# Gate and value products of the last two full token chunks as seven 64x64-tile products, sums accumulated on copies in PSUM, issued from a table

## The chip, the cores and the metric

The kernel runs on one core of a Trainium2 chip. The core has a matrix engine (TensorE, **PE** in the profile; PEld is its weight load), a vector engine (**DVE**), an activation engine (**ACT**), a general engine (**POOL**) and a queue that only issues transfers (**SP**). Engines run side by side and wait for one another through semaphores; each executes its own instructions in order. Products land in PSUM, which has eight banks of 128 partitions x 512 fp32; everything else lies in SBUF. The metric is the time of one execution on the device in microseconds.

## The reference, cut to what matters

An attention block with a feature map of 64 products gives `x`; a gated feed-forward block follows. The change touches the feed-forward block alone.

```python
def phi(x):
    a = np.einsum('rd,bhsd->bhsr', S1, x)
    b = np.einsum('rd,bhsd->bhsr', S2, x)
    return np.einsum('bhsi,bhsj->bhsij', a, b).reshape(*x.shape[:-1], r * r)
# batch 4, heads 4, seq 1088, head_dim 32
num = np.einsum('bhsf,bhfd->bhsd', q_p, kv); den = ...
x = (num / den).transpose(0, 2, 1, 3).reshape(4352, 128)

gate = 1.0 / (1.0 + np.exp(-(x @ w_gate)))     # 4352 x 128 by 128 x 1536
val = x @ w_val                                # 4352 x 128 by 128 x 1536
return gate * val @ w_out                      # 4352 x 1536 by 1536 x 128
```

All is fp32.

## The kernel before, in words

**Tiling.** `xT` holds `x` transposed, 128 features on the partitions and 4352 tokens along them. The tokens are cut into nine chunks: 0 to 7 of 512 tokens, 8 of 256. The 1536 hidden units are twelve blocks j of 128. One *wave* (`w1`, L541) is gate and value of one block j for one chunk: on PE four products (L556), each with 128 rows of contraction and 64 output columns, 512 tokens wide. A product with 64 output columns takes half of PE's columns, so two run beside each other. Then one sigmoid on ACT (L564) and one multiplication on DVE (L599), which writes `g`. The wave's PSUM tile has two banks and two buffers (`psm`). Chunk 8 takes two blocks j in a wave, and its multiplication (L592) also reorders its tokens.

**The output product.** For chunks 1 to 7 two waves make a pair i. The product with `w_out` of a pair (two blocks of 128 hidden units, 128 outputs, 512 tokens as two halves) is done in seven products instead of eight: POOL forms four sums of `g` over token halves (`token_sums`, L371, tile `tsum`), sums of the weights are formed once (`ws`), and PE runs seven products of 128 rows x 64 columns x 256 tokens in `w2_a` and `w2_b` (all through `product`, L381), which add up in the banks `acc0` and `acc1`. After the last pair of a chunk ACT and DVE combine the parts (L486 to L529, L496), DVE transposes (L533) and SP stores (L393). For chunk 8 `w2_end` (L451) runs products of 64 columns with 128 outputs along them, into a bank of `acc0` and one of `ps2`, and `store_end` (L403 to L409) copies the two halves, one on ACT and one on DVE, and stores them from ACT's queue and from SP.

**Order.** Nothing is reordered afterwards on PE, DVE, ACT and POOL: they execute as the Python loop emits. A *slot* (L625) emits the multiplication of the previous wave, then what is due of the output products (a pair's `w2_a` three slots after its second wave, `w2_b` four), then the next wave. Attention of batches 1 to 3 is emitted between slots by a plan of wave numbers (L1352 on); wave 72 is the first of chunk 6, wave 84 the first of chunk 7, and attention has ended by then. `slot(None, 10**3)` emits all the rest. The scheduler of the tile layer sets only SP's order.

**Stores.** Every result tile that is stored uses the tag `o_sb` of pool `sbA`, which has two buffers; the two tiles of `store_end` use it too (L405).

Of the kernel before, what the change touches and what calls it, by code (L numbers as in the profile page):

```python
# [14 lines left out]
MUL = ALU.mult  # L15

P = 128


@with_exitstack  # L20
def kernel(
# [20 lines left out]
    assert DM == H * D == P and D == 32 and R == 8 and S % 32 == 0 and NTOK % 512 == 256  # L42

    T = S // 32

    NJK = 9
    KBASE = [0, 9, 17, 25]
# [10 lines left out]

    dram = ctx.enter_context(tc.tile_pool(name="dram", bufs=1, space=bass.MemoryType.DRAM))

    psm = ctx.enter_context(tc.tile_pool(name="psm", bufs=2, space=bass.MemoryType.PSUM))
    pso = ctx.enter_context(tc.tile_pool(name="pso", bufs=1, space=bass.MemoryType.PSUM))
    ps2 = ctx.enter_context(tc.tile_pool(name="ps2", bufs=1, space=bass.MemoryType.PSUM))

    ctx.enter_context(tc.manual_schedule(
            engines={
# [281 lines left out]

    xT = const.tile([P, NTOK], F32, tag="xT")

    moe = {"sum": -1, "ci": 0, "w": 0, "n": 0, "ready": 0, "acc": None, "gate": None, "todo": [], "late": [], "copies": []}

    def fast(ci):
        return 0 < ci < len(tok_chk) - 1 and tok_chk[ci][1] == TCH

    def weight_sums(n0, n1):
        w = w_sb[:, 2].rearrange("p (n f) d -> p f n d", f=2)[:, :, n0:n1]
# [45 lines left out]
    def store_end(acc):  # L403
        b, r = divmod(tok_chk[-1][0], S)
        o_sb = [sbA.tile([P, P], F32, tag="o_sb", name="o_end") for _ in range(2)]  # L405
        for u, copy in enumerate((nc.scalar.copy, nc.vector.tensor_copy)):
            copy(out=o_sb[u], in_=acc[u])
        for u, eng in enumerate((nc.scalar, nc.sync)):
            eng.dma_start(  # L409
                out=bass.AP(  # L410
                    tensor=out.tensor,
                    offset=out.offset + (b * S + r // 32 + u) * DM,
                    ap=[[T * DM, 32], [2 * DM, 4], [1, DM]],
                ),
                in_=o_sb[u],
            )

    def w2(ci, j0, jn, g):
        if j0 == 0:
            moe["sum"] = ci  # L420
            moe["acc"] = pso.tile([P, TCH], F32, tag="acc0", name="moeout")
        for jj in range(jn):
            j = j0 + jj
            for d in (slice(0, P),) if j < NJ - 1 else (slice(0, 64), slice(64, P)):
                nc.tensor.matmul(  # L425
                    out=moe["acc"][d],
                    lhsT=w_sb[:, 2, j, d],
                    rhs=g[:, jj],
                    start=(j == 0),
                    stop=(j == NJ - 1),  # L430
                )
        if j0 + jn == NJ:
            o_sb = sbA.tile([P, TCH // 32, 32], F32, tag="o_sb", name="o_sb")
            nc.vector.transpose(out=o_sb.rearrange("p t d -> p (t d)"), in_=moe["acc"])
            moe["store"] = lambda: store(
                ci, lambda g4: o_sb[32 * g4 : 32 * g4 + 32], nc.scalar
            )

    def w2_end(ci, j0, jn, g):
        if j0 == 0:  # L440
            moe["sum"] = ci
            moe["acc"] = [
                pso.tile([P, TCH], F32, tag="acc0", name="moeout0")[:, :DM],
                ps2.tile([P, 2, TCH], F32, tag="two", name="moeout1")[:, 0, :DM],
            ]
        acc = moe["acc"]
        for u in range(2):
            for jj in range(jn):
                j = j0 + jj
                for c in (u * P, u * P + 64):  # L450
                    nc.tensor.matmul(  # L451
                        out=acc[u][c % P : c % P + 64],
                        lhsT=g[:, jj, c : c + 64],
                        rhs=w_sb[:, 2, j, :],
                        start=(j == 0),
                        stop=(j == NJ - 1),
                    )
        if j0 + jn == NJ:
            store_end(acc)


    fst = {}

# [31 lines left out]
    def add(out, in0, in1):  # L495
        nc.vector.tensor_tensor(out=out, in0=in0, in1=in1, op=ALU.add)  # L496
# [44 lines left out]
    def w1():  # L541

        ci = moe["ci"]
        t0, tw = tok_chk[ci]
        jn = TCH // tw
        j0 = moe["w"] * jn
        wv = psm.tile([P, 2, TCH], F32, tag="wave", name="wave")

        tp = tw // 2 if ci == 0 and j0 == 0 else tw
        turn = (moe["w"] // 2) % 2  # L550
        for o in range(0, tw, tp):
            for which in range(2):
                for jj in range(jn):
                    for c in (0,) if ci == 0 else (1 - turn, turn):
                        d = slice(0, P) if ci == 0 else slice(64 * c, 64 * c + 64)
                        nc.tensor.matmul(  # L556
                            out=wv[d, which, jj * tw + o : jj * tw + o + tp],
                            lhsT=w_sb[:, which, j0 + jj, d],
                            rhs=xT[:, t0 + o : t0 + o + tp],
                            start=True,  # L560
                            stop=True,
                        )
        sg = sbG.tile([P, TCH], F32, tag="sg", name="sg")
        nc.scalar.activation(out=sg, in_=wv[:, 0], func=ACTF.Sigmoid)  # L564
        if ci == 0:
            if j0 == 0:
                step("final", 2)
                step("sign", 3, bank="acc1")
            if j0 == 1:
                step("final", 3)  # L570
            if 1 < j0 < NJ - 1:
                narrow_w(j0 + 1, 3)
            if j0 > 0:
                narrow_w(j0 + 2, 1)
                narrow_w(j0 + 2, 2)
            if j0 < 3:
                narrow_w(j0 + 3, 0)
            if j0 > 1:
                narrow_w(j0 + 4, 0)
            if j0 == NJ - 3:  # L580
                weight_sums(0, NJ // 4)
            if j0 == NJ - 1:
                weight_sums(NJ // 4, NJ // 2)
        if moe["w"] % 2 == 0:
            moe["g"] = sbG.tile([P, 2, TCH], F32, tag="g", name="g")
        pair, odd, n = moe["g"], moe["w"] % 2, moe["n"]

        def glu():
            g = pair[:, odd]
            todo = moe["todo"]  # L590
            if jn == 2:
                nc.vector.tensor_tensor(  # L592
                    out=g.rearrange("p (j u s y) -> p j y u s", j=2, u=2, y=4),
                    in0=wv[:, 1].rearrange("p (j y u s) -> p j y u s", j=2, u=2, y=4),
                    in1=sg.rearrange("p (j y u s) -> p j y u s", j=2, u=2, y=4),
                    op=MUL,
                )
            else:
                nc.vector.tensor_tensor(out=g, in0=wv[:, 1], in1=sg, op=MUL)  # L599
            if not fast(ci):  # L600
                lag = 4 if ci else 2
                part = (ci, j0, jn, g.rearrange("p (j t) -> p j t", j=jn))
                todo.append((n + lag, lambda: (w2_end if ci else w2)(*part)))
                return
            if not odd:
                moe["t"] = raw.tile([P, 4, HALF], F32, tag="w_in", name="tsum")
            token_sums(pair, moe["t"], odd)
            if odd:
                part = (ci, j0 // 2, pair, moe["t"])
                todo.append((n + 3, lambda: w2_a(*part)))  # L610
                todo.append((n + 4, lambda: w2_b(*part)))

        moe["gate"] = glu
        moe["w"] += 1
        moe["n"] += 1
        if j0 + jn == NJ:
            moe["ci"] += 1
            moe["w"] = 0
# [6 lines left out]
    def slot(group, waves, behind=None):  # L625

        if group is not None:
            group()
        todo = moe["todo"]
        for _ in range(waves):  # L630
            more = moe["ci"] < len(tok_chk)
            if more and sum(tok_chk[moe["ci"]]) > moe["ready"]:
                break
            glu()
            for _ in range(2 if moe["ci"] >= len(tok_chk) - 1 else 1):
                if moe["late"]:
                    moe["late"].pop(0)()
            while todo and todo[0][0] <= moe["n"]:
                todo.pop(0)[1]()
            if behind is not None:  # L640
                behind()
                behind = None
            if more:
                w1()
            for copy in moe["copies"]:
                copy()
            moe["copies"] = []
            if more:
                continue
            if not todo:  # L650
                break
            else:
                todo.pop(0)[1]()

    kT_of, qT_of = {}, {}

# [688 lines left out]
    slot(None, 1)  # L1345
    slot(lambda: parts(1), 1)
    moe["store"]()

    def until(n):
        slot(None, n - moe["n"])  # L1350
# [3 lines left out]
    for b in range(2, B):  # L1354
# [24 lines left out]
        load_kq(b + 1)  # L1379
        until(next(at))  # L1380
        slot(lambda: parts(b), 1)
    slot(None, 10**3)


# [28 lines left out]
```

## Time and profile before

| | us |
|---|---|
| time, median of 3 runs (289.78 to 292.4) | 289.8 |
| span of the profiled execution, first to last instruction | 288.1 |
| PE busy | 282.6 |
| DVE busy | 170.5 |
| POOL busy | 160.0 |
| ACT busy | 106.6 |
| wave products (L556), PE | 201.4 |
| first wave of chunk 6 begins | 207.19 |
| last product of chunk 8 has been issued by | 284.9 |

The profiled execution has no time of its own on the page; its span is the time of the instructions alone, and the median lies 1.7 us above it, for what comes before the first instruction and after the last.

How to read it: a matrix product of fp32 numbers stands as two records, one for each pass. The end of a record is modelled and overlaps with the next one, so durations on PE are taken from start to start. The timeline merges neighbours of one group into a line ("x8"). "128*64 128x512" is 128 rows of contraction, 64 output columns, 512 elements streamed. Groups give busy time, mean ns of one instruction, then the idle time ahead of them with what ended it.

### The profile page before, as it was taken

The page shows a single profiled execution, that of the slowest core. Times are in us where ns is not written, and L with a number is a line of the kernel's source. Part 1 is how long each engine was busy: PE and PEld are TensorE (multiplying, and loading weights), DVE is VectorE, ACT ScalarE, POOL GpSimd, SP SyncE. Part 2 cuts the span into 40 slices and gives each one's busy share as a digit, 9 for nine tenths or more (in the row PEclk, how much of TensorE's full clock was granted, in tenths as well). Part 3 has the DMA queues.
Part 4 walks back from the last instruction along what each step waited for, and adds up shares of the span by engine and source line. Part 5 has one row for each costly group of instructions (what it writes and reads, how often), then busy time and mean ns, then how long its engine had stood idle before and what let it go on. Part 6 is the DMA issues. An engine that isn't in the chain of part 4 may idle for free.

```text
span 288.1 us, 5783 instructions
## 1 busy us (share of the span) xinstructions
PE 282.6 (98%) x2260; PEld 135.1 (47%) x2260; DVE 170.5 (59%) x292; ACT 106.6 (37%) x215; POOL 160.0 (56%) x222
## 2 busy tenths in 40 slices
PE   8899999999999999999999999999999999999995
PEld 4454433354444444535444445444444444444685
DVE  6977788945748547668446485767245223522571
ACT  3688833222334322523244222532243224421341
POOL 2666682667466387383565496483564646555200
PEclk9999999999999999999999999999999999999999
DMA  7995441766500385352000683020001000020012
GB/s 220 348 360 124 104 156 43 171 150 157 164 3 2 77 198 166 92 161 32 1 0 12 162 158 123 2 30 9 0 3 23 14 2 0 4 35 1 0 19 40
DMA packets 28891, 24.24 MB, mean 84 GB/s; under 512 B 18560, under 2 KB 24064, under 8 KB 28864
## 3 DMA queue, kind: packets, MB, share of 16 engines
q1 hardware_dynamic: 25888, 22.10, 30.1%
q10 hardware_dynamic: 2976, 1.77, 2.1%
q8 instruction: 18, 0.29, 0.4%
q14 instruction: 9, 0.07, 0.1%
HBM read 20.60 MB, written 3.26 MB: 83 GB/s over the span
## 4 chain that ended last, share of the span: by engine, by line
PE 97%; ACT 1%; POOL 0%; DVE 0%; issue 0%
PE wave L556 61%; PE prod L381 22%; PE moeout L425 4%; PE moeout L451 2%; PE warm L301 2%; PE kvz L912 1%; PE nps L1270 1%; PE kps L693 1%; PE kvz L899 1%; PE cqps L839 1%; PE nps L1102 0%; PE denj L1041 0%; PE nps L1054 0%; PE dps L1083 0%; ACT asb L810 0%; POOL gh L727 0%
## 5 line engine op out<-in xcount | busy, mean ns | idle before, releaser
L556 PE MATMUL wave<-xT,w_sb 128*64 128x512 f32 (+3 forms) x820 | 201.4, 565 | 0.1
L564 ACT ACTIVATE sg<-wave 128x512 f32<-128x512 f32 x102 | 60.9, 597 | 158.3 <-PE wave L556 152.3
L599 DVE TENSOR_TENSOR g<-wave,sg 128x512 f32<-128x512 f32 x96 | 66.1, 688 | 87.9 <-ACT sg L564 86.3
L371 POOL TENSOR_TENSOR tsum<-g,tsum 128x256 f32<-128x256 f32 x84 | 68.6, 817 | 71.0 <-DVE g L599 70.9
L556 PEld LDWEIGHTS wave<-xT,w_sb 128*64 128x64 f32 (+1 forms) x820 | 71.0, 140 | 72.7 <-issue 53.0
L371 POOL TENSOR_TENSOR tsum<-g 128x256 f32<-128x256 f32 x84 | 66.6, 793 | 22.1 <-DVE g L599 21.5
L381 PE MATMUL prod<-tsum,ws 128*64 128x256 f32 x252 | 68.4, 380 | 0.0
L381 PE MATMUL prod<-g,w_sb 128*64 128x256 f32 (+1 forms) x170 | 50.3, 378 | 0.0
L381 PEld LDWEIGHTS prod<-tsum,ws 128*64 128x64 f32 x252 | 34.0, 137 | 13.1 <-issue 9.7
L381 PEld LDWEIGHTS prod<-g,w_sb 128*64 128x64 f32 x170 | 23.0, 137 | 30.1 <-issue 25.8
L381 PE MATMUL prod<-tsum,w_sb 128*64 128x256 f32 x84 | 25.0, 380 | 0.0
L381 PE MATMUL prod<-g,ws 128*64 128x256 f32 x84 | 25.0, 379 | 0.0
L162 POOL TENSOR_TENSOR head<-head,tail 128x384 int32<-128x384 int32 (+1 forms) x13 | 13.2, 1023 | 4.4 <-DVE head L157 4.4
L381 PEld LDWEIGHTS prod<-g,ws 128*64 128x64 f32 x84 | 11.5, 137 | 5.7
L425 PE MATMUL moeout<-g,w_sb 128*128 128x512 f32 (+1 forms) x26 | 12.4, 596 | 0.0
L381 PEld LDWEIGHTS prod<-tsum,w_sb 128*64 128x64 f32 x84 | 11.3, 137 | 1.3 <-issue 1.0
L592 DVE TENSOR_TENSOR g<-wave,sg 128x512 f32<-128x512 f32 x6 | 6.8, 1134 | 6.3 <-ACT sg L564 4.7
L772 DVE TENSOR_TENSOR kp<-kab 128x1152 f32<-128x1152 f32 (+1 forms) x8 | 10.2, 1289 | 0.0
L892 DVE TENSOR_TENSOR qp<-qp,bq 128x1152 f32<-128x1152 f32 (+1 forms) x7 | 10.1, 1444 | 0.0
L496 DVE TENSOR_TENSOR res<-prod,other 128x256 f32<-128x256 f32 x14 | 5.9, 425 | 6.3 <-ACT other L487 4.8
L141 POOL TENSOR_SCALAR head<-cap 128x384 f32<-128x384 f32 (+1 forms) x13 | 6.2, 483 | 4.6 <-ACT cap L140 4.6
L152 ACT ACTIVATE tail<-w_in,two__157 128x384 f32<-128x384 uint32 (+1 forms) x12 | 7.3, 618 | 0.0
(130 smaller groups left out, 197.5 us busy)
## 6 DMA issues: line engine op xcount, KB each, us to landing
qp<-dq SPq DMA_DIRECT2D x7, 576.0 KB
bq<-dq SPq DMA_DIRECT2D x14, 288.0 KB
kq<-in_k_dram SPq DMA_DIRECT2D x3, 544.0 KB
kq<-in_q_dram SPq DMA_DIRECT2D x3, 544.0 KB
w_in<-in_moe_w_out_dram SPq DMA_DIRECT2D x6, 256.0 KB
w_in<-in_moe_w_gate_dram SPq DMA_DIRECT2D x5, 256.0 KB
w_in<-in_moe_w_val_dram SPq DMA_DIRECT2D x5, 256.0 KB
v<-in_v_dram SPq DMA_DIRECT2D x8, 144.0 KB
```

What stands on the lines that cost most here:

```text
L141: nc.gpsimd.tensor_scalar(out=self.head.bitcast(F32), in0=self.cap, scalar1=122880.0, scalar2=2.0**-15, op0=ALU.min, op1=ALU.max,)
L152: nc.scalar.activation(out=self.tail, in_=self.lo, func=ACTF.Identity, bias=two, scale=2.0**-51)
L162: nc.gpsimd.tensor_tensor(out=self.head, in0=self.head, in1=self.tail.bitcast(I32), op=ALU.add)
L371: nc.gpsimd.tensor_tensor(out=t[:, u], in0=in0, in1=in1, op=ALU.subtract)
L381: nc.tensor.matmul(out=out, lhsT=lhsT, rhs=rhs, start=start, stop=stop, skip_group_check=True)
L425: nc.tensor.matmul(out=moe["acc"][d], lhsT=w_sb[:, 2, j, d], rhs=g[:, jj], start=(j == 0), stop=(j == NJ - 1),)
L556: nc.tensor.matmul(out=wv[d, which, jj * tw + o : jj * tw + o + tp], lhsT=w_sb[:, which, j0 + jj, d], rhs=xT[:, t0 + o : t0 + o + tp], sta ...
L564: nc.scalar.activation(out=sg, in_=wv[:, 0], func=ACTF.Sigmoid)
L592: nc.vector.tensor_tensor(out=g.rearrange("p (j u s y) -> p j y u s", j=2, u=2, y=4), in0=wv[:, 1].rearrange("p (j y u s) -> p j y u s", j ...
L599: nc.vector.tensor_tensor(out=g, in0=wv[:, 1], in1=sg, op=MUL)
L772: eng.tensor_tensor(out=KP[b][:, pi, j0:j1].rearrange("p j m (i l) -> p (j m) i l", i=R), in0=bass.AP(tensor=a0.tensor, offset=a0.offset, ...
L892: nc.vector.tensor_tensor(out=q0, in0=q0, in1=half(BQ[b], n), op=MUL)
```

## The change

For chunks 6 and 7 gate and value of one block j are now taken as one product of two row halves (64 features each) by two column parts (gate, value) by two token halves, and formed by seven products instead of eight. Each is 64 rows x 128 columns x 256 tokens, issued as two of 64 x 64 (`feature`, items P1 to P7; a prime marks the second of the two blocks of a unit w, twelve units w for both chunks).

- **Inputs.** `cross_weights` copies weight halves to the other row half by 24 transfers on SP and forms the weight sums with 72 subtractions and additions of 64x128 on POOL, two to a slot from wave 21 on. `load_y` copies the tokens of a chunk so that both row halves hold both feature halves (four transfers each), and `x_sum` forms four differences of 128x256 on DVE for each chunk.
- **Sums in PSUM.** ACT copies the bank of P1 to the bank of P6 and P7 (Aa) and the bank of P5 to SBUF (Ac); P6 accumulates on the copy; DVE adds that and the copy of P5 back into P5's bank (D1), on which P3 accumulates; P7 accumulates on the first; DVE adds again, into SBUF (D2), and P4 accumulates on the first. Then come two sigmoids (Sa, Sc) and two multiplications (M1, M2), all 128x512.
- **Output products.** The same seven products of a pair, but cut into row halves of 64 rows (WL, WU), or whole (WF) near the end. The last two pairs of chunk 5 are held back and issued here.
- **Order.** From wave 72 on everything on PE, DVE, ACT and POOL is issued as the table `ORDER` lists it, chunk 8 (C, Y, Z, O) and the closing of chunks 5 to 7 (E, F) too. Odd units swap the row halves. Closing a chunk uses ACT copies, small transfers on SP, and DVE (`empty`, `total`).
- **PSUM.** Pools `psm` and `ps2` are closed at the start of this section and six single banks opened in their place.

```diff
+ORDER = """
+WLB:-2.0 WUA:-2.1 WUA:-2.0 P1':0 P1':1 P1:0 P1:1 P5:0 T0:1 Aa:0 P5:1 P5':0 P5':1 Aa:1 P2':0 P6':0
+P2:0 Ac:0 P6:0 P6':1 Ac:1 P2:1 P6:1 D1:0 WLA:-2.0 P2':1 D1:1 P7:0 P3':0 Sa:1 P3:0 P7':0 Sa:0 P7:1
...
+WFB:9.0 WFB:11.0 WFB:10.0 O1:2 O2:5 EB:1 O1:4 O2:2 O1:1 O2:1 O3:3 O3:0 O3:1 F0:1 O3:2 O2:0 F1:1 O0:1
+O2:4 O2:3 O3:4 O1:0 O0:3 F2:1 O0:2 O1:5 F3:1 O0:4 F4:1 O3:5 O0:5 F5:1 O0:0 O1:3 F6:1
+"""
+    SECT, HELD, PREP, BUF = 6, 2, 20, 0
...
+    def cross_weights():
+        for j in range(NJ):
+            f, (lead, tail) = fw[j], halves(j // 2)
+            nc.sync.dma_start(out=f[lead, :2], in_=w_sb[tail, :2, j])
+            if j // 2 % 2 == 0:
+                nc.sync.dma_start(out=f[tail, ::2], in_=w_sb[lead, :2, j])
+            else:
+                nc.sync.dma_start(out=f[tail, 2], in_=w_sb[lead, 1, j])
...
+                if ci == SECT - 1 and j0 // 2 >= NJ // 2 - HELD:
+                    moe["held"].append(part[2:])
+                    return
...
+            for _ in range(2 if moe["n"] > PREP else 0):
+                if moe["prep"]:
+                    moe["prep"].pop(0)()
...
+        GA, GC, V = (bank[4], bank[BUF]), (bank[5], bank[BUF + 1]), (bank[2 - BUF], bank[3 - BUF])
...
+        def feature(k, nn, w):
+            lead, tail = halves(w)
...
+            rows, lhsT, rhs, dst = {
+                "P1": (lead, gate if even else f[:, 0], y[:, 0, :HALF], GA),
+                "P2": (lead, f[:, 0] if even else gate, y[:, 1, :HALF], GA),
+                "P5": (lead, f[:, 1], s[:, 0], GC),
+                "P3": (lead, f[:, 2], y[:, 1, HALF:], GC),
+                "P6": (tail, f[:, 0], s[:, 1], V),
+                "P7": (tail, f[:, 1], s[:, 2], V),
+                "P4": (tail, val if even else f[:, 2], s[:, 3], V),
+            }[k]
+            start = k in ("P1", "P5") and (k, w) not in started
+            for c in range(2):
+                product(
+                    dst[w % 2][half_of(c), nn * HALF : (nn + 1) * HALF],
+                    lhsT[rows, half_of(c)], rhs[rows], start, False,
+                )
...
+            if k == "Aa":
+                nc.scalar.copy(out=v, in_=ga)
+            elif k == "Ac":
+                nc.scalar.copy(out=s5, in_=gc)
...
+            elif k == "D1":
+                add(gc, v, s5)
+            elif k == "D2":
+                add(c2, v, s5)
+            elif k == "M1":
+                nc.vector.tensor_tensor(out=g[:, :, first], in0=two(v), in1=sg[:, :, first], op=MUL)
+            else:
+                nc.vector.tensor_tensor(out=g[:, :, second], in0=two(c2), in1=sg[:, :, second], op=MUL)
...
+        def empty(b, c):
...
+            nc.scalar.copy(out=e, in_=acc[b, c])
+            if b == "A":
+                nc.sync.dma_start(out=x1[LO], in_=e[HI, :HALF])
+                nc.sync.dma_start(out=x1[HI], in_=e[LO, :HALF])
+            else:
+                nc.sync.dma_start(out=x2[LO], in_=e[HI, HALF:])
+                for rows in (LO, HI):
+                    nc.sync.dma_start(out=x5[rows], in_=e[LO, HALF:])
...
+        def total(u, c):
...
+                    (r0, a[:, :HALF], x1),
+                    (r0, r0, a[:, HALF:]),
+                    (y[LO, :HALF], b[LO, :HALF], a[LO, :HALF]),
+                    (y[HI, :HALF], b[HI, :HALF], r0[HI]),
+                    (y[LO, :HALF], y[LO, :HALF], x2[LO]),
+                    (y[:, HALF:], r0, x5),
...
+            o_sb = sbA.tile([P, TCH // 32, 32], F32, tag="o_sb", name="o_sb")
+            nc.vector.transpose(out=o_sb.rearrange("p t x -> p (t x)"), in_=y)
+            store(SECT + c, lambda g4: o_sb[32 * g4 : 32 * g4 + 32])
...
+                    acc["end"] = [pso.tile([P, TCH], F32, tag="acc0", name="moeout0")[:, :DM], V[0][:, :DM]]
...
+        store_end(acc["end"])
...
-    slot(None, 10**3)
+    at = NJ * SECT
+    until(at - 2)
+    load_y(0)
+    load_y(1)
+    until(at - 1)
+    x_sum(0, 0)
+    x_sum(0, 1)
+    until(at)
+    glu()
+    x_sum(0, 2)
+    x_sum(0, 3)
+    for x in moe["late"]:
+        x()
+    section()
```

Other items of the table: T is `x_sum` of the second chunk, Q a sum of `token_sums`, C the gate and value products of chunk 8 (128 rows), Y its sigmoid, Z its multiplication, O its output products, E `empty`, F `total` (F6 is the transpose and the store).

## The prediction

> **What bounds the kernel now.** I read the chain that ended last first, from the page.
>
> ```profile
> ## 4 chain that ended last, share of the span: by engine, by line
> PE 97%; ACT 1%; POOL 0%; DVE 0%; issue 0%
> ```
>
> PE sets the end nearly alone, so work taken off PE counts in full as long as nothing else becomes late. The next view is PE's timeline where chunk 6 begins: start, length, engine, line, operation, number of records.
>
> ```profile
> 207.19 1.89 PE L556 MATMUL wave<-xT,w_sb 128*64 128x512 f32 x8
> 208.90 0.38 PE L381 MATMUL prod<-g,w_sb 128*64 128x256 f32 x1
> ...
> 209.55 0.38 PE L381 MATMUL prod<-tsum,ws 128*64 128x256 f32 x1
> ...
> 209.76 1.89 PE L556 MATMUL wave<-xT,w_sb 128*64 128x512 f32 x8
> ```
>
> Start to start, a wave of four products takes 208.90 - 207.19 = 1.71 us: two side by side, two passes each, four steps of 0.43. The 256-wide products behind it start in pairs 0.21 to 0.22 us apart, so a step costs half when it is half as wide. I call 0.43 us, two 256-wide passes on all four quarters of PE, a **slot**. There is no gap between the lines. Third, the groups (busy time, mean ns, idle time ahead).
>
> ```profile
> L564 ACT ACTIVATE sg<-wave 128x512 f32<-128x512 f32 x102 | 60.9, 597 | 158.3 <-PE wave L556 152.3
> L599 DVE TENSOR_TENSOR g<-wave,sg 128x512 f32<-128x512 f32 x96 | 66.1, 688 | 87.9 <-ACT sg L564 86.3
> L371 POOL TENSOR_TENSOR tsum<-g,tsum 128x256 f32<-128x256 f32 x84 | 68.6, 817 | 71.0 <-DVE g L599 70.9
> L592 DVE TENSOR_TENSOR g<-wave,sg 128x512 f32<-128x512 f32 x6 | 6.8, 1134 | 6.3 <-ACT sg L564 4.7
> ```
>
> All three engines wait for PE. They have room, and their durations price the new steps.
>
> **Products removed (-4.9 us).** Before, 24 waves of chunks 6 and 7 cost 24 x 1.71 = 41.0 us. After, twelve units have 14 items P each, 168 items of half a slot: 84 slots x 0.43 = 36.1. The output products keep their number; cut into row halves they again fill a slot by twos. I counted the table: in every slot an item of the upper rows stands with one of the lower rows, so none is half empty. This needs four tiles at work together. A 64-row mode is in the trace:
>
> ```profile
> 95.97 0.71 PE L693 MATMUL kps<-kT,sk 64*32 64x288 f32 x16
> 96.48 0.69 PE L839 MATMUL cqps<-qT,skq 64*32 64x288 f32 x16
> 97.10 0.43 PE L381 MATMUL prod<-tsum,w_sb 128*64 128x256 f32 x1
> ```
>
> Sixteen records, eight tiles with two passes each, take 0.51 us; 288 columns in two passes alone take 0.43 x 288/256 = 0.48. So row halves and column quarters run side by side. Issue is no limit: the change needs 8 records in 0.43 us (54 ns each), and this line has 16 in 0.51 (32 ns each).
>
> The Trainium skill has a rule against this change: "TensorEngine Tiling (Array Packing)", section "Performance Considerations", gives every matmul an overhead of some 60 cycles on trn2. Taken as 25 ns added to each of 168 narrower passes in a row (an estimate from that page), it would eat 4.2 of the 4.9 us; the rows of 0.43 against 0.21 to 0.22 contradict it, and I add nothing.
>
> **Mode changes (+0.5).** The two 288-wide groups should take 0.48 each; the second, followed by a change back to 128 rows, takes 0.62. The difference, 0.11 to 0.14, is one change. The table has four (entry, into and out of chunk 8, chunk 8 again): 4 x 0.12.
>
> **Entry (+0.2).** The two column halves of PE end half a slot apart before the new section; the first slot waits for both.
>
> **Copies and adds on the path (+0.7).** Per unit (about 4.5 us of PE), ACT has two copies (0.59 each, row asb of L810, 128x512 out of PSUM) and two sigmoids (0.60): 2.4 us. DVE has D1, D2, M1, M2 at 0.69: 2.8. POOL has four sums at 0.73 to 0.82: about 3. No engine is full; what counts is latency. Mostly three slots, 1.30 us, stand in the table between the last P6 and the P7 or P3 that needs D1, and as many between P7 and P4, which needs D2. D1 needs 0.15 (from PE's last issue to the start on ACT or DVE, as from 284.76 to 284.91 below) + 0.69 + 0.05 = 0.89: 0.4 us of slack, PE staying busy meanwhile. Aa hides likewise. D1 writes PSUM, which no DVE row of before does. Ends: 0.6 and 1.13 (the strided multiplication of L592); I take 0.69, the row with the same 128x512 and one PSUM input.
>
> M2 reads two SBUF tiles, and so do the sums on POOL. The trace shows what happens to such pairs:
>
> ```profile
> 103.41 1.35 DVE L772 TENSOR_TENSOR kp<-kab 128x1152 f32<-128x1152 f32 x1
> 103.57 1.78 POOL L371 TENSOR_TENSOR tsum<-g 128x256 f32<-128x256 f32 x1
> ```
>
> The sum, usually 0.73, took 1.78 us: it stood still until DVE was done. The Trainium skill, "SBUF — State Buffer", section "Who interferes with whom", makes this an exclusive lock for DVE instructions with two SBUF inputs, held by whoever issued first; so M2 could be the one that waits, which no row of this trace shows.
>
> If M2 starts while a sum runs (POOL busy 48 x 0.73 = 35 of 74 us, so about half the time), it loses 0.37 on average: 12 x 0.5 x 0.37 = 2.2 us of delay on DVE, up to 12 x 0.73 = 8.8, down to 0. Queued behind M2 is the next unit's D1 or D2, and behind that P3, P7 or P4. The 0.4 us of slack takes most of it; I keep a third, 0.7, with 0 to 3 as its range.
>
> **Before wave 72 (0).** 24 transfers on SP, 72 operations of 64x128 on POOL (0.73 for 256 wide and 0.6 for 192 wide in the trace, so I estimate 0.45 each, 32 us) in waves 21 to 57, eight copies of tokens, eight DVE differences (0.43 each, L496). POOL is at 16 to 18 of 29 us per stage there and rises to about 26; a sum has 1.5 to 2 us before the products need it. If that cover goes, +0.5. The transfers pass SP ahead of later loads; the nearest needed one has 1 us of room, so again 0 to 0.5.
>
> **Tail (+2.4).** The end of before, by time:
>
> ```profile
> 284.48 0.27 ACT L407 COPY o_end<-moeout 128x128 f32<-128x128 f32 x1 [2.38 <-PE moeout L451]
> 284.77 0.66 ACTq L409 DMA_DIRECT2D out_dram<-o_end  x1
> 284.91 0.29 DVE L407 COPY o_end<-moeout 128x128 f32<-128x128 f32 x1 [1.67 <-PE moeout L451]
> 285.23 0.64 SPq L409 DMA_DIRECT2D out_dram<-o_end  x1
> ```
>
> The last product is issued by T = 284.76 (its last record starts 0.11, one 128-wide step, before); the span ends at 288.1, T + 3.35, of which 2.9 follow SP's issue. The two tiles of `store_end` share tag `o_sb` with chunk 7's result. In the changed order the pool gives both tiles the same buffer, and DVE's copy must wait until ACT's transfer has landed; before, they lay in two. The transfer engines carry nothing until 286.0, then both tiles at a share of 0.45 until 287.0; so the first has landed at about 286.5, some 1.8 us from its issue. So: T + 0.15 + 0.27 + 0.02 + 1.8 + 0.05 + 0.29 + 0.03 + 2.9 = T + 5.5, that is +2.15. Chunk 7's four stores are issued by SP from about T - 0.4 on, later than before (279.11), and share the transfer engines with ACT's: 0 to 0.8, taken 0.3. Ends of the step: 0.4 (landing hidden) and 3.3.
>
> **Sum.** -4.9 + 0.5 + 0.2 + 0.7 + 0 + 2.4 = -1.1. The profiled execution's span of 288.1 becomes 287.0; the median shown lies 1.7 above the span, so 289.8 becomes **288.7 us**. Over 1% (2.9 us) is what a measurement here can tell from no change, so I forecast no change that counts, slightly on the fast side.
>
> **Rivals.**
>
> 1. *The tail is not serial, or M2 costs nothing* (0.18). The stores land sooner than the rows of before suggest, or slack hides them. For: the wait is one transfer of 64 KB. Against: that data moved only after 286.0. Tail at 0.6, lock at 0.2: -4.9 + 0.5 + 0.2 + 0.2 + 0.6 = -3.4, 286.4 us.
>
> 2. *DVE becomes the bound* (0.19, the slower side). D1, reading PSUM and SBUF and writing PSUM, takes 1.13 as L592 does. Then 0.15 + 1.13 + 0.05 = 1.33 exceeds three slots (it breaks from 1.10), twice per unit for D1 and D2, and what M2 loses is no longer absorbed: DVE has 2 x 1.13 + 2 x 0.69 = 3.6 of 4.5 us. Of 24 adds each loses 0.03 to 0.1, plus M2's 2.2: about 3.8 in place of 0.7, so +2.0, 291.8 us. If M2 always meets a sum, +5 to +8. For: everything on DVE is in one order, and P7, P3 and P4 of both units hang on it. Against: only the strided row has 1.13.
>
> 3. *The change does not do what it says* (0.03): opposite row halves don't run together for 64x64 tiles. Then about 133 slots take twice 0.43: +57 us, 346 us. The rows of 64x32 speak against it.
>
> **Chances.** Forecast 0.60, rivals 0.18, 0.19, 0.03. The first three lie within 286 to 292.5, which leaves out the last and the bad half of the second. Faster than 286.9: most of rival 1 and a little of the forecast, 0.22. Slower than 292.7: the bad half of rival 2 and rival 3 with a little of the forecast's loss terms, 0.18. Rest 0.60.
>
> **What would show it.** In the changed profile: PE busy from wave 72 on with slots 0.43 apart, 64*64 records four at a time; idle on PE ended by DVE only in a few places, in all below 1 us (right) or above 3 (rival 2); D1 near 0.7 or near 1.1; a DVE wait of about 1.8 us ended by a DMA before the last copy, and an end 5 to 6 us after the last product; POOL sums that stretch beyond 1 us, or M2 that does. A sigmoid or copy on ACT that waits for a PSUM bank, a product that waits for the copies made by `load_y`, or a result chunk's small transfers on the path of `total` would make it wrong in ways not priced here.

## The result and the profile after

The changed kernel takes **294.11 us** (median of 4 runs, 293.44 to 294.63) against 289.88 us before: ratio **1.0136, 95% interval 1.0093 to 1.0179**. The forecast was 288.7 us, with 286.0 to 292.5 as range. The measured time lies above that range, and the kernel became slower where a little faster was forecast. The profiled execution has a span of 292.8 us beside 288.1: 4.7 us to explain. It is the longest of the four, and executions of this kernel differ by 1.2 us; so sums over profiles below hold for this one, and the medians are the firmer numbers. The granted clock of both profiles is 1.00 until PE's last product, so the clock is not the cause.

The page of the changed kernel, the chain that ended last, its first line:

```profile
PE 61%; POOL 17%; DVE 7%; DMA 5%; issue 3%; SPq 2%; ACT 2%; ACTq 1%; POOLq 0%; DVEq 0%
```

Before, this line said PE 97%. Now POOL holds 17% and the transfers with their queues 8%. The span falls apart into three stretches, each read from starts of PE's records (T is the start of the last record and one step of 0.11 us):

| us | before | after | after without the weight sums (a_nosum) |
|---|---|---|---|
| third batch's `denj` products (L1041, L1089, L1088) begin | 192.58 | 196.50 | 192.87 |
| first 64x64 product (entry of the new section) | - | 210.77 | 207.15 |
| entry to PE's last product | - | 74.7 | 74.7 |
| PE's last product issued (T) | 284.7 | 285.5 | 281.9 |
| span end | 288.1 | 292.8 | 289.2 |
| end behind T | 3.4 | **7.3** | 7.4 |

The difference at the entry is taken as the cost of the weight sums: in this execution they cost 210.77 - 207.15 = 3.6 us and the tail 7.3 - 3.4 = 3.9, and without them PE would end 284.7 - 281.9 = 2.8 earlier than before: 3.6 + 3.9 - 2.8 = 4.7. The 3.6 is at the upper end: in the five profiles with the same preparation the entry lies between 209.2 and 210.8, that is 2.1 to 3.6 us behind a_nosum.

**The new section does what it should.** PE and DVE of the changed kernel at its entry (timeline: start, length, engine, line, operation):

```profile
210.77 0.43 PE L462 MATMUL prod<-tsum,ws 64*64 64x256 f32 x1
...
211.49 0.38 PE L462 MATMUL prod<-tsum,ws 64*64 64x256 f32 x1
211.50 0.69 DVE L649 TENSOR_TENSOR g<-wave,sg 128x512 f32<-128x512 f32 x1 [1.81 <-ACT sg L622]
...
212.25 0.43 PE L462 MATMUL b<-yt,w_sb 64*64 64x256 f32 x2 [0.39 <-DVE g L649]
```

One wait of 0.55 us at the entry: the first P1 comes only after the last wave's multiplication. After it no wait of PE above 0.1 us stands in the section, except for the four mode changes (0.12 to 0.13 each, at 210.7, 261.3, 264.9 and 267.2). Groups of the section, 210 to 268 us:

```profile
L554 DVE TENSOR_TENSOR b<-b,s 128x512 f32<-128x512 f32 x12 | 8.4, 699 | 4.4 <-PE b L462 3.0 <-ACT s L1542 1.0
L554 DVE TENSOR_TENSOR c<-b,s 128x512 f32<-128x512 f32 x12 | 8.2, 689 | 1.6 <-PE b L462 1.1
...
L1554 DVE TENSOR_TENSOR g<-c,sg 128x512 f32<-128x512 f32 x12 | 10.6, 883 | 1.3 <-ACT sg L1546 0.6 <-PE prod L462 0.4
L1552 DVE TENSOR_TENSOR g<-b,sg 128x512 f32<-128x512 f32 x11 | 7.6, 689 | 1.3 <-PE b L462 1.0
```

D1, which writes PSUM, takes 0.70 us, as taken. M2 (L1554, two SBUF inputs) takes 0.88 where M1 (L1552, one input in PSUM) takes 0.69: it loses 0.19 on average to the sums on POOL, and DVE still waits for PE. Row by row it takes 0.68 to 0.69 in the four places where no sum runs at its start, or one is about to end, and 0.71 to 1.22 in the other eight, the more the longer the running sum still has to go. Without a sum, and behind one that ended at 241.43:

```profile
264.90 0.69 DVE L1554 TENSOR_TENSOR g<-c,sg 128x512 f32<-128x512 f32 x1
240.76 1.22 DVE L1554 TENSOR_TENSOR g<-c,sg 128x512 f32<-128x512 f32 x1
```

**Before the section POOL has little room.** Busy time in two stretches of 42 us, before first, then the changed kernel (columns PE, PEld, DVE, ACT, POOL, clock, transfers):

```profile
85.00:127.00 42.00, 42.00 (x356) 19.34 (x354) 28.42 (x44) 15.11 (x32) 26.57 (x32) 1.00 0.40 96
127.00:169.00 42.00, 42.00 (x322) 18.65 (x320) 23.84 (x39) 13.26 (x25) 23.45 (x31) 1.00 0.31 73
```

```profile
85.00:127.00 42.00, 41.51 (x350) 18.84 (x347) 33.18 (x43) 14.99 (x32) 40.06 (x60) 1.00 0.39 92
127.00:169.00 42.00, 41.42 (x312) 17.90 (x311) 24.07 (x39) 12.99 (x24) 38.03 (x66) 1.00 0.26 63
```

POOL goes from 26.6 to 40.1 of 42 us, and in the first stretch DVE, whose instructions there are the same but for the shift in time, from 28.4 to 33.2. PE's waits from 60 to 207 us of the changed kernel have a line that the kernel before does not have:

```profile
PEld prod L462 <- POOL tsum L452: 4.5, 11, 1.2
```

(4.5 us in 11 waits, the longest 1.2; part of it is hidden under products already running.) One such place, the timeline of the changed kernel:

```profile
172.73 0.46 POOL L429 TENSOR_TENSOR fw<-w_sb,fw 64x128 f32<-64x128 f32 x1
172.96 1.31 DVE L994 TENSOR_TENSOR z<-kp 128x1024 f32<-128x1024 f32 x1
173.14 1.44 POOL L429 TENSOR_TENSOR fw<-w_sb,fw 64x128 f32<-64x128 f32 x1
...
174.66 0.73 POOL L452 TENSOR_TENSOR tsum<-g 128x256 f32<-128x256 f32 x1
...
175.47 0.46 POOL L429 TENSOR_TENSOR fw<-fw 64x128 f32<-64x128 f32 x1
...
176.00 0.79 POOL L429 TENSOR_TENSOR fw<-w_sb 64x128 f32<-64x128 f32 x1
...
176.76 0.71 POOL L452 TENSOR_TENSOR tsum<-g,tsum 128x256 f32<-128x256 f32 x1
...
177.44 0.72 POOL L452 TENSOR_TENSOR tsum<-g 128x256 f32<-128x256 f32 x1
177.53 0.43 PE L462 MATMUL prod<-tsum,ws 128*64 128x256 f32 x1 [0.70 <-POOL tsum L452]
```

An operation of the preparation takes 0.46 us alone; the one that starts at 173.14, while DVE works with two SBUF inputs, takes 1.44 and ends 0.3 behind DVE. The token sum behind them is late, and PE waits for it: the records before and after that wait are 1.09 us apart, 0.87 more than a step.

**The tail is SP's queue.** The end of the changed kernel:

```profile
278.75 0.59 ACT L1578 COPY e<-prod 128x512 f32<-128x512 f32 x1 [4.58 <-PE prod L462]
...
281.92 0.48 SPq L1580 DMA_DIRECT2D xb<-e  x1
...
284.60 0.43 DVE L554 TENSOR_TENSOR r<-e,xb 128x256 f32<-128x256 f32 x1 [6.76 <-DMA xb<-e]
...
287.09 0.71 DVE L1601 STREAM_TRANSPOSE o_sb<-y 128x512 f32<-128x512 f32 x1
287.83 1.95 SPq L474 DMA_DIRECT2D out_dram<-o_sb  x4
288.11 0.29 DVE L488 COPY o_end<-b 128x128 f32<-128x128 f32 x1 [0.31 <-DMA out_dram<-o_end]
289.88 0.63 SPq L490 DMA_DIRECT2D out_dram<-o_end  x1
```

Half of chunk 7's result lay in SBUF from 279.3 (ACT's copy of `acc0`, 278.75 + 0.59), but its first small transfer left SP at 281.9. From 277.9 to 281.8 SP issued eight stores of chunk 6, whose tokens lie in two sequences:

```profile
277.86 3.96 SPq L474 DMA_DIRECT2D out_dram<-o_sb  x8
```

So DVE's closing chain began at 284.6, chunk 7's stores at 287.8, and the last result had to go behind them on SP. The wait for the shared buffer, which the forecast had as 2.15 us, is the 0.31 in the line of 288.11.

### The profile page after: what moved, and what is told of

The parts are those of the page before. It is cut to its first block, busy times and chain, and to the rows that moved or that the text cites. A ratio compares the mean times of both kernels' runs of the same rounds, so it can differ in the third digit from the quotient of the medians.

```text
span 292.8 us, 7262 instructions
## 1 busy us (share of the span) xinstructions
PE 280.9 (96%) x2880; PEld 149.9 (51%) x2880; DVE 204.0 (70%) x327; ACT 115.0 (39%) x224; POOL 197.5 (67%) x294
## 4 chain that ended last, share of the span: by engine, by line
PE 61%; POOL 17%; DVE 7%; DMA 5%; issue 3%; SPq 2%; ACT 2%; ACTq 1%; POOLq 0%; DVEq 0%
PE wave L614 24%; PE b L462 16%; PE prod L462 12%; POOL tsum L452 9%; POOL fw L429 8%; PE moeout L506 3%; DMA bq<-dq 3%; DVE g L649 2%; SPq L474 1%; ACTq L474 1%; PE nps L1318 1%; ACT sg L622 1%; DMA s_in<-in_S_dram 1%; DVE xT L1352 1%; DMA out_dram<-o_end 1%
## 5 line engine op out<-in xcount | busy, mean ns | idle before, releaser
L614 PE MATMUL wave<-xT,w_sb 128*64 128x512 f32 (+2 forms) x532 | 142.0, 590 | 0.6 <-DVE g L649 0.4
L649 DVE TENSOR_TENSOR g<-wave,sg 128x512 f32<-128x512 f32 x72 | 49.2, 685 | 43.3 <-ACT sg L622 43.0
L462 PE MATMUL prod<-tsum,ws 128*64 128x256 f32 (+1 forms) x312 | 78.4, 380 | 0.9 <-POOL tsum L452 0.7
L462 PE MATMUL prod<-g,w_sb 128*64 128x256 f32 (+2 forms) x210 | 53.2, 377 | 0.0
L462 PEld LDWEIGHTS prod<-tsum,ws 128*64 128x64 f32 (+1 forms) x312 | 39.6, 135 | 17.9 <-issue 9.4
L462 PE MATMUL b<-yt,fw 64*64 64x256 f32 x528 | 42.4, 377 | 0.0
L462 PEld LDWEIGHTS prod<-g,w_sb 128*64 128x64 f32 (+1 forms) x210 | 24.9, 135 | 13.9 <-issue 9.9
L462 PEld LDWEIGHTS b<-yt,fw 64*64 64x64 f32 x528 | 27.2, 133 | 6.4 <-ACT b L1540 0.5
L462 PE MATMUL prod<-g,ws 128*64 128x256 f32 (+1 forms) x104 | 30.2, 379 | 0.0
L462 PE MATMUL prod<-tsum,w_sb 128*64 128x256 f32 (+1 forms) x104 | 30.0, 379 | 0.0
```

The lines of the kernel that those rows point to most:

```text
L462: nc.tensor.matmul(out=out, lhsT=lhsT, rhs=rhs, start=start, stop=stop, skip_group_check=True)
L614: nc.tensor.matmul(out=wv[d, which, jj * tw + o : jj * tw + o + tp], lhsT=w_sb[:, which, j0 + jj, d], rhs=xT[:, t0 + o : t0 + o + tp], sta ...
```

## The experiments

Medians, with the ratio to the kernel before as measured beside it. The columns entry, T and tail are of the profiled run, a single execution.

| run | us | ratio (95%) | entry | T | tail |
|---|---|---|---|---|---|
| changed kernel | 294.1 | 1.0136 (1.0093 to 1.0179) | 210.8 | 285.5 | 7.3 |
| once more | 293.6 | 1.0132 (1.0107 to 1.0157) | 209.2 | 284.0 | 7.4 |
| b_prep | 293.5 | 1.0123 (1.0097 to 1.0150) | - | 288.1 | 3.4 |
| b_xfer | 290.8 | 1.0031 (1.0005 to 1.0058) | - | 286.9 | 3.4 |
| a_nosum | 292.3 | 1.0084 (1.0056 to 1.0112) | 207.1 | 281.9 | 7.4 |
| a_spread | 292.0 | 1.0074 (1.0053 to 1.0095) | 207.9 | 282.6 | 7.4 |
| a_dve | 295.8 | 1.0192 (1.0154 to 1.0230) | 211.6 | 286.3 | 7.3 |
| a_oend | 294.3 | 1.0126 (1.0093 to 1.0160) | 210.5 | 285.2 | 7.4 |
| a_st | 293.0 | 1.0098 (1.0063 to 1.0134) | 209.4 | 284.1 | 6.1 |
| a_tail | 291.1 | 1.0054 (1.0024 to 1.0085) | 209.9 | 284.6 | 4.9 |
| best1 | 289.3 | 0.9973 (0.9958 to 0.9987) | 207.6 | 282.3 | 4.6 |
| best2 | 291.9 | 1.0060 (1.0038 to 1.0082) | 210.7 | 285.5 | 4.7 |
| best3 | 288.9 | 0.9971 (0.9951 to 0.9992) | 207.3 | 282.1 | 5.1 |

In every one of the eleven profiles with the new section, entry to T is 74.7 or 74.8 us; all differences lie before and behind it.

### The preparation alone, and its transfers alone

`cross_weights` and its place in `slot` were put into the kernel before (b_prep); then without the operations on POOL (b_xfer).

```diff
+            for _ in range(2 if moe["n"] > 20 else 0):
+                if moe["prep"]:
+                    moe["prep"].pop(0)()
...
     moe["store"]()
+    cross_weights()
```

> The kernel before, with the weight preparation of the change alone added (24 transfers on SP, 72 operations of 64x128 on POOL, two to a slot from wave 21 on; nothing reads the result). Theory A, POOL overfilled: in the changed profile PE does work for 161.1 of 167.7 us up to the new section, 6.6 lost, against 2.2 of 164.2 before; the preparation alone costs the difference of 4.4 us, so about 294 us. Rival B, something else in those waves (copies of tokens, differences on DVE, the held pairs, PSUM banks): within 0.7 us of the kernel before, about 290.

> The kernel before with the 24 transfers of the weight preparation on SP alone, without the operations on POOL. Theory A (POOL overfilled): nothing, 289.9 us within 0.4. Rival B2, the transfers stand ahead of later loads on SP or take the transfer engines from them: 1 us or more, 291.

Measured: b_prep 293.5 us, +3.5; its waits of PE near 127, 128, 138 and 177 (0.32, 0.20, 0.55 and 0.87 us) are those of the changed kernel at the same places. One of 0.37 near 67 is in after2, a_nosum and, with 0.7, in a_spread too. Its waits for POOL's token sums are those of the changed kernel, and b_xfer has none:

```profile
PEld prod L428 <- POOL tsum L418: 4.4, 10, 1.2
```

Theory A holds, at 3.5 and not 4.4. The transfers alone cost 0.9 in the median, between the two expectations. The profiled run of b_xfer lost 1.9 us in its first 16 us, before any of these transfers (last section), and only 0.3 after; what the 0.9 of the median consists of was not traced. So 0.3 to 0.9 of the 3.5 are the transfers, and the rest is POOL's operations.

### The changed kernel without the sums

```diff
-            nc.sync.dma_start(out=f[lead, :2], in_=w_sb[tail, :2, j])
+            nc.sync.dma_start(out=f[lead], in_=w_sb[tail, :, j])
...
-            moe["prep"] += sums()
```

> The changed kernel without the 72 operations of 64x128 on POOL; the same 24 transfers fill the weight tiles with unsummed halves instead, so the weight sums of the seven products are left out. Theory A: 294.1 - 4.4 = 289.7 us, PE without waits for POOL's token sums before wave 72. Rival B: 294 us, unchanged.

The 24 transfers move more here, 72 blocks of 64x128 in place of 42, as each fills all three parts of a half. In the profile the entry comes 3.6 us earlier, nearly as A has it, and span and T follow; PE has no wait for POOL's token sums left. The median falls by 1.8 only: its ten runs lie between 291.0 and 295.4 and the profiled one is the fastest, while the changed kernel's profile is the slowest of its runs. That spread was not explained, so the size of the loss is better taken from b_prep.

### Where the operations go: on DVE, or three in two slots

```diff
-                    lambda o=o: nc.gpsimd.tensor_tensor(
+                    lambda o=o: nc.vector.tensor_tensor(
```

```diff
-            for _ in range(2 if moe["n"] > PREP else 0):
+            for _ in range((2 if moe["n"] % 2 else 1) if moe["n"] > PREP else 0):
```

> The changed kernel with the 72 preparing operations on DVE in place of POOL. Theory A1, POOL's room is what is missing (40.1 of 42 us busy): POOL falls back to about 27 of 42, most of the 4.4 us return, about 291.5. Rival A2, the two engines keep each other out whenever both read SBUF, so that moving the operations only moves the wait to the attention's chain on DVE: 294 or more.

> The changed kernel with three preparing operations in two slots in place of four, so that they end at wave 69 and not at 57. Theory A1: POOL has 4 x 0.73 + 3 x 0.56 = 4.6 us of work in two slots of about 4.9, where four gave 5.2; the stalls fall by half or more, about 292. Rival A2: the same operations meet the same DVE instructions, about 294.

a_spread: 292.0, as A1 says; the entry is at 207.9, 0.7 behind the kernel without the sums. Its stretches:

```profile
85.00:127.00 42.00, 42.00 (x354) 19.22 (x352) 29.35 (x44) 15.29 (x33) 37.89 (x54) 1.00 0.41 92
127.00:169.00 42.00, 42.00 (x322) 18.85 (x320) 24.40 (x40) 13.28 (x25) 34.91 (x57) 1.00 0.31 75
```

The same operations, with 4 and 7 us of room on POOL, cost PE next to nothing in these two stretches. a_dve: 295.8, the rival A2. POOL falls to 23.4 us, but DVE rises to 38.7 and 37.8, and PE now waits for DVE:

```profile
PEld wave L614 <- DVE g L649: 5.4, 9, 1.8
```

```profile
92.32 0.70 DVE L429 TENSOR_TENSOR fw<-w_sb,fw 64x128 f32<-64x128 f32 x1
...
97.66 0.29 DVE L429 TENSOR_TENSOR fw<-fw 64x128 f32<-64x128 f32 x1
```

An operation takes 0.26 to 0.29 us alone on DVE and mostly 0.7 to 0.8 where it meets a sum on POOL; together they take 36.4 us, hardly less than the 39.8 on POOL. So it is not POOL as such: either engine stretches the other's instructions, and the engine that gets all 72 in a row has little time left to catch up a delay. In a_spread the operations are stretched as much (38.9 us in all); what differs is the room between them. The busy share alone sets no limit: a_spread loses next to nothing with POOL at 37.9 of 42 us, the changed kernel 0.6 with 38.0 in its second stretch. How often a sum that is needed soon comes late was not varied by itself.

### The tail: the buffer, the closing of chunk 6, SP's issues

a_oend gives the last two tiles buffers of tag `sg`. a_st moves `F2:0` to `F6:0` in the table behind `Z:3` and `Z:2`. a_tail does both and lets ACT's queue issue half of chunk 6's stores, one of chunk 7's, and the two `xpd` transfers of chunk 7.

```diff
-        o_sb = [sbA.tile([P, P], F32, tag="o_sb", name="o_end") for _ in range(2)]
+        o_sb = [sbG.tile([P, TCH], F32, tag="sg", name="o_end")[:, :P] for _ in range(2)]
```

```diff
-M1:11 Q1:10 C1:3 C0:3 Q0:11 C3:3 Y:3 C2:3 Q2:10 C0:2 Z:3 Q1:11 C1:2 C2:2 Y:2 Q2:11 C3:2 C0:5 Z:2
+M1:11 Q1:10 C1:3 C0:3 Q0:11 C3:3 Y:3 C2:3 Q2:10 C0:2 Z:3 F2:0 F3:0 Q1:11 C1:2 C2:2 Y:2 Q2:11 C3:2 C0:5 Z:2 F4:0 F5:0 F6:0
...
```

> The changed kernel with the last two result tiles in two buffers of their own. Theory C (SP's queue): DVE's last copy waited only 0.3 us for the transfer, and SP's last issue then stood behind four stores until 289.9 anyway: 0 to 0.3 us, about 294.0. Rival D, the forecast's own step (the shared buffer costs 2.15 us): about 292.

> The changed kernel with the last five closing steps of chunk 6 moved up in the table, between chunk 8's multiplications. Theory C, SP's queue sets the end: chunk 6's eight stores (277.9 to 281.8) stand ahead of chunk 7's small transfers, whose sources are ready from 279.3; moved ahead by about 3 us they let chunk 7's closing end about 2.4 us earlier: about 291.7 us. Rival D, the shared buffer of the last two results sets the end: unchanged, 294.1.

> The changed kernel with the closing of chunk 6 moved up, the last two result tiles in buffers of their own, and a part of SP's issues on ACT's queue: half of chunk 6's stores, one of chunk 7's, two of chunk 7's small transfers. Theory C (SP's queue in order): the end comes about 4.3 us after PE's last product, not 7.3 as in the changed kernel or 6.1 with the closing alone moved; about 291.1 us. Rival: the chain copy, transfer, six additions, transposition, store of chunk 7 is itself that long, so not below 292.5.

a_oend: 294.3, tail 7.4: the shared buffer alone costs nothing here. a_st: tail 6.1; 1.3 us (1.1 in the medians) of the 2.4 expected. Chunk 7's stores come 1.8 us earlier against T (284.6 with T at 284.1, 287.8 with 285.5 before), the last issue 1.3, because what was hidden now counts. Its end:

```profile
284.62 0.69 ACTq L490 DMA_DIRECT2D out_dram<-o_end  x1
286.90 0.29 DVE L488 COPY o_end<-b 128x128 f32<-128x128 f32 x1 [2.33 <-DMA out_dram<-o_end]
287.22 0.63 SPq L490 DMA_DIRECT2D out_dram<-o_end  x1
```

DVE waits 2.33 us for the shared buffer, and SP's last issue comes 0.55 us after SP had room for it (284.60 + 2.07 = 286.67): the wait that cost nothing costs 0.55 here. And chunk 6's stores still held SP until 278.6, 0.6 us after chunk 7's first half was ready (277.9). a_tail: 291.1, as expected, with a tail of 4.9 where 4.3 was expected:

```profile
284.40 1.41 SPq L474 DMA_DIRECT2D out_dram<-o_sb  x3
284.86 0.27 ACT L488 COPY o_end<-moeout 128x128 f32<-128x128 f32 x1 [4.63 <-PE moeout L462]
285.15 0.64 ACTq L490 DMA_DIRECT2D out_dram<-o_end  x1
285.89 0.55 ACTq L474 DMA_DIRECT2D out_dram<-o_sb  x1
285.91 0.69 SPq L490 DMA_DIRECT2D out_dram<-o_end  x1
```

Both queues now start their last issues together, 1.3 us behind T.

### Both repairs together

best1 is a_spread with a_tail, two of chunk 7's stores on each queue. best2 and best3 also move weight transfers (sixteen, eight) from SP to ACT's queue, one to a slot behind the sigmoid.

```diff
+                if j < 8:
+                    nc.sync.dma_start(out=o, in_=i)
+                else:
+                    moe["move"].append(lambda o=o, i=i: nc.scalar.dma_start(out=o, in_=i))
```

> The changed kernel with both repairs: three preparing operations in two slots, and the closing of chunk 6 moved up, own buffers for the last two tiles, SP's issues shared with ACT's queue (now two of chunk 7's stores each). If the two losses are independent: 294.1 - 3.0 (closing) - 2.1 (preparation) - 0.3 = 288.7 us, below the kernel before by 1.1. If both only shift the same wait: about 290.5.

> The same with the weight transfers of blocks 4 to 11 issued from ACT's queue, one to a slot, in place of all 24 from SP in a row. In the run before with three operations in two slots, batch 1's gathers left SP at 53.0 in place of 50.8, DVE waited 2.4 us for one of them, and PE 0.7 us: that goes, 288.2 us. Rival: the stall near 67.5 has another cause, or ACT's issues delay sigmoids: 288.7 or more.

> Both repairs, and only the weight transfers of blocks 8 to 11 (eight of 24) from ACT's queue, one to a slot; they end near 96, before the place near 112 where ACT stood 4 us ahead of such an issue. Sixteen transfers leave SP by about 49, before batch 1's gathers at 50.5. If SP's delay of the gathers makes the stall near 67.5 and nothing else comes: 289.3 - 0.3 = 289.0 us. Rival: ACT's issues cost elsewhere as well, 289.3 or more.

> The changed kernel once more, beside these two on one chip: 294.1 us, PE's last product near 285.5 and the end 7.3 us behind it, if the profile of the first run was typical.

best1: 289.3 us where 288.7 was expected, faster than the kernel before by 0.27% (0.13 to 0.42). a_spread and a_tail alone took off 2.1 and 3.0 us, both together 4.8, so the losses are close to independent. best2: the stall near 67.5 (0.7 us in a_spread, but only 0.2 in best1 with the same preparation) is gone, and another came: ACT, executing in order, was through with a sigmoid at 112.6, stood until 116.5 ahead of one weight transfer and until 119.9 ahead of the next:

```profile
116.46 0.49 ACTq L412 DMA_DIRECT2D fw<-w_sb  x1
117.05 0.60 ACT L627 ACTIVATE sg<-wave 128x512 f32<-128x512 f32 x1 [4.47 <-PE prod L467]
119.88 0.60 ACTq L412 DMA_DIRECT2D fw<-w_sb  x1
120.52 0.37 ACT L989 COPY kvd<-kvz 128x256 f32<-128x256 f32 x1 [2.87 <-DMA b<-dq]
```

PE waited for that copy and lost 2.6 us there. The profile ends ACT's wait with a transfer of the attention (`b<-dq`); why a weight transfer has to wait for it, the trace does not show. best3 avoids it: 288.9, with an interval that overlaps that of best1, so that moving eight transfers helped is not shown. after2 repeats the result; its entry came 1.5 us earlier than in the first profile, its tail and section did not move.

## Why the prediction was wrong, point by point

- **Products removed (-4.9), mode changes (+0.5), entry (+0.2).** Right, but for the entry, where the first P1 waits another 0.55. With the sums left out PE ends 2.8 us earlier; -4.9 + 0.5 + 0.2 + 0.55 is -3.65. Another 0.3 is lost by 192.9 already (192.87 against 192.58). The remaining 0.5 was not traced. The Trainium skill's overhead per matmul ("TensorEngine Tiling (Array Packing)", "Performance Considerations"), which would have eaten 4.2 us, did not show: 64x64 records of 256 columns start a step of 0.21 us apart.
- **Copies and adds on the path (+0.7).** No such stall is in the section. M2 lost 2.3 us in all, as forecast (2.2), but the 0.4 us of slack took all of it. The open question of the lock's direction is answered: M2 is held too, where a sum is already running (0.71 to 1.22 for 0.69). This agrees with the Trainium skill, "SBUF — State Buffer", "Who interferes with whom", which lets whoever issued first keep the port.
- **Before wave 72 (0).** This step failed, by 3.5 us in b_prep and 2.1 to 3.6 in the profiles. It took 0.45 us for an operation and compared POOL's sum over a stage with the stage's length. The sum was nearly right: 40.1 and 38.0 of 42 us are 27.7 and 26.3 of 29, where about 26 was forecast. It is a wrong measure: an operation does take 0.46 alone, but 0.55 on average and up to 1.46, and with POOL busy for 95% and 91% of the stretches a delay by a long DVE instruction reaches the sums behind it, until PE waits for one (at 177.53). The cover named, 1.5 to 2 us ahead of each sum, was gone there; the cost without it was put at 0.5. b_prep shows the cost, b_xfer that the transfers are the smaller part, and a_nosum and a_spread that it goes with the operations or with more room between them.
- **Tail (+2.4).** It was +3.9, and the reason given was wrong, not the size only. The shared buffer cost nothing in the changed kernel (a_oend), since SP's queue was later still. The forecast moved chunk 7's closing to T - 0.4 without following SP's queue ahead of it: chunk 6 has eight stores, issued from 277.9 on. Behind them the small transfers, six additions, four stores and the last result stand in a row. The forecast's own list of signs names small transfers on the path of `total` as something it had not priced.
- **Rival 2**, DVE as the bound by D1 at 1.13 us, named 291.8 us on the slower side, but not by what happened: D1 takes 0.70, and PE lost nothing to it. Rival 1 had it right that M2 costs PE nothing, and the tail wrong. Rival 3 is excluded by the section's 74.7 us.

The terms with what the profiles measured: -4.9 + 0.5 + 0.2 + 0.55 + 0.3 + 0 + 3.6 + 3.9 = +4.15, beside +4.7 of the spans (0.5 not traced) and +4.2 of the medians.

## What to carry to other kernels

Preparing work on a helper engine is not free because its sum fits: look at how near to full the engine gets in that stretch, and at which long instructions of its neighbour it must meet; spreading three operations over two slots took back 2.1 us of what two in each cost. A queue that issues transfers executes in order as well: when results move to the end, write down everything that it has to issue in the last 10 us, with the durations of its rows. And a wait found in the program may cost nothing while another one is later; it counts once the other is removed (a_st).

## What the runs showed of the hardware that was not expected

- Early products can take 1.7 times as long with no lower clock granted. In b_xfer's profiled run, with the granted clock at 1.00:

```profile
7.42 1.16 PE L849 MATMUL aps<-qT,s 32*64 32x256 f32 x16
```

against, before,

```profile
6.93 0.69 PE L800 MATMUL aps<-qT,s 32*64 32x256 f32 x16
```

  It ended by 16 us and left that execution 1.9 us behind. None of the other 13 profiles has it; its cause stays open. The Trainium skill ("TensorE: Matmul & The Clock Gate", "Part 1: The HAM clock gate") describes a start at half rate that varies from run to run; the clock row here, 1.00 in these 16 us, shows nothing of it.
- DVE and POOL stretch each other both ways: a 64x128 addition of 0.26 to 0.29 us on DVE mostly becomes 0.7 to 0.8 beside a sum on POOL, one of 0.46 on POOL 1.44 beside a long DVE instruction.
- A small store lands 2.0 to 2.3 us after its issue (286.02 to 288.1, 284.62 to 286.9), not the 1.8 worked out from the shares of the transfer engines.
